# Turning the first chunks of x on TensorE at the head of a fused attention and FFN kernel

## The chip, the cores and the metric

The kernel runs on one core of a Trainium2 chip. The metric is the device time of one execution in microseconds (us). Before the change it is 286.64 us, the median of 3 runs (286.60 to 286.99). The profile below is of one more execution.

## The reference

The input x has 2048 tokens of 640 features. Two branches are computed from it and mixed by a gate for each token. Branch A is a linear attention with 32 heads of width 20; branch B is a gated FFN of width 1728.

```python
x = A_x
g = _sigmoid((x * gate_w).sum(-1, keepdims=True))
# a: q, k, v = x @ wqkv; features of q and k are softmax(p) and softmax(-p), p = q @ w_phi;
#    kv = sum over tokens of features x v; a = (phi_q @ kv) / (phi_q @ z) @ wo
# b: (silu(x @ w_gate) * (x @ w_up)) @ w_down
return g * a + (1 - g) * b
```

All tensors are bfloat16 in HBM. TensorE contracts over the partitions, so both branches need x with its features on the partitions: xT, five chunks of 128 features by 2048 tokens.

## The kernel before

**Tiling.** The tokens are worked in four blocks of 512 (`bt`) for the FFN and in sixteen tiles of 128 (`t`) for the attention. The FFN's 1728 columns are cut into 13 pieces of 128 and one of 64 (`k`). For one block and one piece the gate is five matmuls of 512 columns, one for each chunk of x, into a PSUM bank, and the up part is five more into another. A tail follows: ScalarE computes a tanh of the gate (hT) and a scaled copy of up (us), VectorE combines gate and tanh (L665), POOL multiplies (L671, called hmul). Groups `down` and `rest` then multiply hT with w_down. In the attention a k tile and later a q tile goes through `p1` or `p0` (projection), VectorE's max, min and two subtractions, ScalarE's exp, VectorE's sum and reciprocal, POOL's normalization (L983). For a q tile the features are transposed by a DMA (eT), multiplied with kv (`num`), divided on VectorE (L1066 to L1076), transposed by a DMA (oT) and multiplied with w_o (`wo`). The `rest` group's result is transposed by a DMA too (rX).

**What sets the order.** `_Plan` is a list scheduler that runs while the program is built. Each task has an engine, a cost, a priority, tasks it depends on and pools it takes from (8 PSUM banks among them); a load has a time at which it is said to land. The planner walks through its own time and puts each task on its engine's instruction list when it could start. On the chip each engine then runs its list in order; `_Tracker` adds a semaphore wait where data or a buffer needs one. A task whose cost or landing time is changed can so change the order of others much later. All loads and transposing DMAs stand on one queue, SP's; `load` (with `after`) keeps the loads in the order of their priorities.

**The beginning.** TensorE starts with filler matmuls on a constant (`warm`, L618 to L630): four on banks 0 to 3, then six on banks 4 to 7, 4 and 5. They compute nothing that is used. Then comes the head (`ffn_head`, L694): the gate and up parts of the first four pieces for the first 512 tokens, ordered by what has been loaded rather than piece by piece. Its first group multiplies chunks 0 and 1 of x with four pieces of w_gate, eight matmuls in one task, into four banks; the second does the same with w_up; then come chunks 2 to 4. The loads stand in this order on SP (L547 to L553): w_gate's rows of chunks 0 and 1 for 512 columns; x's chunks 0 and 1 for the first 512 tokens, transposed by the DMA; w_up's rows of chunks 0 and 1; w_gate's rows of chunks 2 to 4 for the first two pieces; x's chunks 2 and 3, and 4, transposed by the DMA; w_gate's other rows; w_up's other rows. POOL meanwhile sets pads and builds masks (L604, L607), and ScalarE loads its table.

Of the kernel before, what the change touches and what calls it, by code (L numbers as in the profile page):

```python
# [6 lines left out]
P = 128  # L7
S_TOK = 2048
D = 640
H = 32  # L10
DH = 20
F_FFN = 1728
NT = S_TOK // P
# [16 lines left out]
NPC_W = 6  # L30
PHI_NH = (6, 6, 6, 6, 6, 2)
ACTF = mybir.ActivationFunctionType
ALU = mybir.AluOpType
AX = mybir.AxisListType
DT = mybir.dt
BF16 = DT.bfloat16
# [204 lines left out]
class _Plan:  # L241
# [11 lines left out]
    def add(self, eng, cost, fn, deps=(), prio=5.0, lat=None, acq=(), rel=(), name=""):  # L253
        t = _Task(eng, cost, fn, deps, prio, self.LAT[eng] if lat is None else lat,
                  tuple(acq), tuple(rel), len(self.tasks), name)
        self.tasks.append(t)
        return t
# [82 lines left out]
def _mm(*cols):  # L340
    return sum(c / 2400.0 + 0.003 for c in cols)


def _build(
# [13 lines left out]
    pe, act, dve, pool, sp = nc.tensor, nc.scalar, nc.vector, nc.gpsimd, nc.sync  # L358
    run = tr.run

    def rowelems(shape):
        r = 1
        for s_ in shape[1:]:
            r *= s_
        return r

    def sb(name, shape, dtype):
        t = nc.alloc_sbuf_tensor(name, list(shape), dtype)
        tr.reg_tensor(t, "sbuf", nc.lookup_mloc(t).addr, rowelems(shape), mybir.dt.size(dtype))
        return t  # L370

    def sbat(name, shape, dtype, at):
        t = nc.alloc_sbuf_tensor_at(name, list(shape), dtype, offset=at)
        tr.reg_tensor(t, "sbuf", at, rowelems(shape), mybir.dt.size(dtype))
        return t

    xT = sb("xT", [P, 5, S_TOK], BF16)
# [33 lines left out]
    base = nc.lookup_mloc(slab).addr  # L411
# [2 lines left out]
    wqT = sbat("wqT", [P, 2 * NPC_W, D], BF16, base)  # L414
    wbd = sbat("wbd", [P, NPC_W, 6, DH], BF16, base + 2 * NPC_W * D * 2)
    wph = sbat("wph", [PC, NPC_W, DH], BF16, base + 2 * NPC_W * D * 2 + NPC_W * 6 * DH * 2)

    ps = nc.alloc_psum_tensor("ps", [P, 8 * 512], F32)
    tr.addr[ps.name] = ("psum", 0, 8 * 512, 4)

    x2 = A_x[0]
# [3 lines left out]
    add = plan.add  # L425
# [4 lines left out]
    def one(b, c0, c1, r0=0, r1=P):  # L430
        return ps[r0:r1, b * 512 + c0:b * 512 + c1]
# [4 lines left out]
    def mms(groups):  # L436

        reads = [g[1] for g in groups] + [g[2] for g in groups]
        writes = []
        seen = set()  # L440
        for g in groups:
            k = (g[0].offset, str(g[0].ap))
            if k not in seen:
                seen.add(k)
                writes.append(g[0])

        def fn():
            last = None
            for o, l, r, st, sp_ in groups:
                last = pe.matmul(o, lhsT=l, rhs=r, start=st, stop=sp_, skip_group_check=True)  # L450
            return last
        run("pe", fn, reads=reads, writes=writes)
# [5 lines left out]
    def actop(o, i, func, scale=1.0):  # L458
        reads = [i] + ([scale] if isinstance(scale, bass.AP) else [])
        run("act", lambda: act.activation(o, i, func, scale=scale), reads=reads, writes=[o])  # L460

    def dveop(fn, reads, writes):
        run("dve", fn, reads=reads, writes=writes)

    def poolop(fn, reads, writes):
        run("pool", fn, reads=reads, writes=writes)

    def memset(t_ap, val, eng):
        eobj = {"pool": pool, "dve": dve}[eng]
        run(eng, lambda: eobj.memset(t_ap, val), reads=[], writes=[t_ap])  # L470
# [3 lines left out]
    def dma(eng, dst, src, transpose=False, keep=False):  # L474
        eobj = tr.engobj[eng]
        reads = [src] if src.tensor.name in tr.addr else []
        writes = [dst] if dst.tensor.name in tr.addr else []
        fn = (lambda: eobj.dma_start(dst, src, transpose=True)) if transpose else (lambda: eobj.dma_start(dst, src))
        ev = run(eng, fn, reads=reads, writes=writes, semname="dma")
        if keep:  # L480
            out_evs.append(ev)
# [12 lines left out]
    def load(eng, dst, src, land, prio, transpose=False, name="load", cost=0.06):  # L494

        t = add(eng, cost, lambda: dma(eng, dst, src, transpose=transpose), prio=prio, lat=2.0, name=name)
        t.land = land
        t.slack = L_SLACK if land > 13 else 0.0
        t.after = chain.get(eng)
        chain[eng] = t  # L500
        return t
# [7 lines left out]
    wgl = [None] * (NPC + 1)  # L509
    wul = [None] * (NPC + 1)  # L510

    def load_gu(j, eng, land, prio):
        c0, c1 = PIECES[j]
        wgl[j] = load(eng, wg[:, :, c0:c1], gsrc[:, :, c0:c1], land[0], prio)
        wul[j] = load(eng, wu[:, :, c0:c1], usrc[:, :, c0:c1], land[1], prio + 0.1)

    def load_x(bt, prio, *cuts):

        tok = slice(512 * bt, 512 * bt + 512)
        out_ = []  # L520
        for i, (c0, c1, land) in enumerate(cuts):
            out_ += [load("sp", xT[:, c0:c1, tok], x2[tok, c0 * P:c1 * P], land, prio + 0.1 * i, True, "x%d" % bt)] * (c1 - c0)
        return out_
# [13 lines left out]
    xs = [None] * NBT  # L537
    HD = 4
    hw = {}

    def load_head(key, c0, c1, k0, k1, land, prio):
        w, src = (wg, gsrc) if key == "g" else (wu, usrc)
        t = load("sp", w[:, c0:c1, k0 * P:k1 * P], src[:, c0:c1, k0 * P:k1 * P], land, prio)
        for k in range(k0, k1):
            hw[key, c0, k] = t
        return t
    load_head("g", 0, 2, 0, HD, 3.9, -43)  # L547
    xa = load_x(0, -42, (0, 2, 5.25))
    load_head("u", 0, 2, 0, HD, 6.9, -41)
    load_head("g", 2, 5, 0, 2, 7.4, -40.5)  # L550
    xs[0] = xa + load_x(0, -40, (2, 4, 8.8), (4, 5, 9.3))
    wgl[0] = load_head("g", 2, 5, 2, HD, 10.0, -39.5)
    wul[0] = load_head("u", 2, 5, 0, HD, 11.3, -39)  # L553
    load_gu(1, "sp", (12.5, 13.7), -37)
    xs[1] = load_x(1, -36.5, (0, 5, 16.4))
    phi_rows = A_w_phi.rearrange("h e f -> (h e) f")
# [16 lines left out]
    xl = [x_[4] for x_ in xs]  # L573

    zero = add("dve", 0.3, lambda: memset(us[:, 0, 0:2], 0.0, "dve"), prio=-20, name="zero")
    table = add("act", 1.3, lambda: actop(us[:, 1, 0:1], us[:, 0, 0:1], ACTF.Tanh), deps=[zero], prio=-20, name="table")
# [39 lines left out]
    def warm(banks, before):  # L618
        ctx = {}

        def fn():
            for b in banks:
                last = pe.matmul(one(b, 0, 512), lhsT=ones_row[:, 0:P], rhs=ones_row[:, 0:512], start=True, stop=True, skip_group_check=True)  # L623
            return last
        b0, b1 = min(banks), max(banks) + 1
        t = add("pe", 0.427 * len(banks), lambda: run("pe", fn, reads=[], writes=[ps[:, b0 * 512:b1 * 512]]), prio=-10,
                acq=[("bank", ctx, i) for i in range(b0, b1)], rel=[("bank", ctx, i) for i in range(b0, b1)], name="warm")
        t.after = before
        return t
    warm_t = warm((4, 5, 6, 7, 4, 5), warm((0, 1, 2, 3), None))  # L630


    gate_t = {}
# [60 lines left out]
    def ffn_head():  # L694
        tsl = slice(0, 512)
        cs = [{} for _ in range(HD)]
        before = warm_t
        last = {}

        def group(key, c0, c1, parts):  # L700
            nonlocal before
            w = wg if key == "g" else wu

            def fn(ks, cc):
                mms([(one(cs[k][key], 0, 512), w[:, c, P * k:P * k + P], xT[:, c, tsl], c == 0, c == 4) for c in cc for k in ks])
            for ks in parts:
                t = add("pe", _mm(*[512] * (len(ks) * (c1 - c0))), lambda ks=ks: fn(ks, range(c0, c1)),
                        deps=[xs[0][c1 - 1], hw[key, min(c0, 2), ks[-1]]], prio=-5,
                        acq=[("bank", cs[k], key) for k in ks] if c0 == 0 else (), name="head")
                t.after = before  # L710
                before = t
                for k in ks:
                    last[key, k] = t
        group("g", 0, 2, [(0, 1, 2, 3)])
        group("u", 0, 2, [(0, 1, 2, 3)])
        group("g", 2, 4, [(0, 1)])
        group("g", 4, 5, [(0, 1)])
        group("g", 2, 5, [(2, 3)])
        group("u", 2, 5, [(0,), (1,), (2,), (3,)])
        for k in range(HD):  # L720
            ffn_tail(0, k, cs[k], (last["g", k], last["u", k]), 0)
# [372 lines left out]
    pre_q = premult(0, wqT_l, PRE_Q, 0.02)  # L1094
    wq_done[0] = pre_q[-1]
    ffn_head()
    for bt in range(NBT):
        for t in range(4 * bt, 4 * bt + 4):
# [5 lines left out]
    for bt in range(1, NBT):  # L1104
        ks = list(range(K_PAIRS if bt == 1 else 0, NK))
# [74 lines left out]
```

## Time and profile before

| | us |
|---|---|
| median of the runs | 286.64 (286.60 to 286.99) |
| the profiled execution's own time | 286.7 |
| its span, from the first to the last instruction | 285.0 |
| TensorE busy in the span | 281.9 (99%) |
| VectorE busy | 225.8 (79%) |
| POOL busy | 172.4 (61%) |
| ScalarE busy | 150.2 (53%) |

The profile is one execution, with times from the span's start. PE is TensorE's matmuls, PEld its weight loads, DVE VectorE, ACT ScalarE, POOL GpSimd, and SPq the issuing of DMAs on SP's queue. A line such as L450 is a line of the kernel; since one helper issues all matmuls, it is the tiles behind it (`ps<-xT,wg`) that tell the groups apart. A matmul is pipelined: its shown duration reaches beyond the start of the next, so that paces are read from start to start. In the first 6.2 us the sixteen DMA engines move 158 GB/s on average.

### The profile page before, as it was taken

The numbers are of one execution on the slowest core, as the hardware profiler recorded it, in microseconds if no ns is written. First come the engines' busy times: TensorE is split into PE (matmuls) and PEld (weight loads), VectorE is DVE, ScalarE is ACT, GpSimd is POOL, SyncE is SP. The second block draws the span as 40 slices with busy tenths as digits, with TensorE's granted clock in tenths as the row PEclk, the third lists the DMA queues.
The fourth block names the chain that finished last, engine by engine and source line by source line (L and its number), as shares of the span: only waits on it lengthen the run. The fifth ranks groups of instructions, "written<-read, shape, count | busy, mean of one in ns | idle before, by whom it ended". The sixth has DMA issues, their size and how long they took to land.

```text
span 285.0 us, 4720 instructions
## 1 busy us (share of the span) xinstructions
PE 281.9 (99%) x1816; PEld 143.4 (50%) x1816; DVE 225.8 (79%) x326; ACT 150.2 (53%) x242; POOL 172.4 (61%) x170
## 2 busy tenths in 40 slices
PE   8999999999999999999999999999999999999996
PEld 3445554555554544555455455455555554554544
DVE  1323449998999797997999999999998989982132
ACT  2455655886676564345761655366655454563210
POOL 5099633749478637366498286588888643867100
PEclk9999999999999999999999999999999999999999
DMA  7979998940000000000002344444344544535211
GB/s 169 264 124 232 231 234 121 307 140 0 0 2 0 2 18 0 2 0 18 2 1 54 74 97 92 100 102 97 74 99 98 116 100 96 69 63 115 48 46 64
DMA packets 70431, 24.73 MB, mean 87 GB/s; under 512 B 58569, under 2 KB 70409, under 8 KB 70409
## 3 DMA queue, kind: packets, MB, share of 16 engines
q1 hardware_dynamic: 69753, 24.43, 40.2%
q8 instruction: 14, 0.23, 0.3%
q10 hardware_dynamic: 656, 0.00, 0.1%
q14 instruction: 8, 0.07, 0.1%
HBM read 8.30 MB, written 2.62 MB: 38 GB/s over the span
## 4 chain that ended last, share of the span: by engine, by line
PE 99%; DVE 0%; issue 0%
PE ps L450 97%; PE ps L623 2%; DVE xsb L760 0%
## 5 line engine op out<-in xcount | busy, mean ns | idle before, releaser
L671 POOL TENSOR_TENSOR hT<-hT,us 128x512 bf16<-128x512 bf16 (+1 forms) x56 | 64.0, 1154 | 52.3 <-DVE hT L665 31.9
L983 POOL TENSOR_TENSOR phi<-phi,rc 128x1320 bf16<-128x1320 bf16 x32 | 77.6, 2426 | 23.6 <-DVE rc L977 23.6
L450 PE MATMUL ps<-xT,wg 128*128 128x512 bf16 x280 | 69.6, 381 | 0.0
L450 PE MATMUL ps<-xT,wu 128*128 128x512 bf16 x260 | 64.3, 379 | 0.0
L665 DVE SCALAR_TENSOR_TENSOR hT<-hT,ps 128x512 bf16<-128x512 bf16 (+1 forms) x56 | 37.6, 677 | 23.4 <-ACT hT L460 23.3
L460 ACT ACTIVATE phi<-phi 128x1320 bf16<-128x1320 bf16 x32 | 41.7, 1303 | 22.6 <-DVE phi L962 22.6
L973 DVE TENSOR_REDUCE sm<-phi 128x66 f32<-128x1320 bf16 x32 | 48.2, 1510 | 5.5 <-ACT phi L460 5.5
L460 ACT ACTIVATE hT<-ps 128x512 bf16<-128x512 f32 (+1 forms) x56 | 33.0, 595 | 37.1 <-PE ps L450 36.9
L450 PE MATMUL ps<-wd,hT 128*128 128x512 bf16 (+2 forms) x238 | 50.7, 366 | 0.0
L450 PE MATMUL ps<-wkv,xT 128*128 128x289 bf16 (+2 forms) x240 | 45.6, 343 | 0.0
L460 ACT ACTIVATE us<-ps 128x512 bf16<-128x512 f32 (+1 forms) x56 | 33.2, 597 | 15.5 <-PE ps L450 13.5
L450 PEld LDWEIGHTS ps<-xT,wu 128*128 128x128 bf16 x260 | 25.4, 98 | 30.7
L450 PEld LDWEIGHTS ps<-xT,wg 128*128 128x128 bf16 x280 | 25.9, 98 | 27.3 <-issue 1.5
L450 PEld LDWEIGHTS ps<-wd,hT 128*128 128x128 bf16 x238 | 22.4, 98 | 24.0
L450 PEld LDWEIGHTS ps<-wkv,xT 128*128 128x128 bf16 x240 | 23.1, 97 | 19.4
L950 DVE TENSOR_REDUCE mx<-ps 128x33 f32<-128x660 f32 x32 | 26.5, 830 | 2.9 <-PE ps L450 2.9
L962 DVE TENSOR_TENSOR phi<-mn,ps 128x660 bf16<-128x660 f32 x32 | 26.6, 831 | 0.5
L954 DVE TENSOR_REDUCE mn<-ps 128x33 f32<-128x660 f32 x32 | 26.5, 829 | 0.0
L958 DVE TENSOR_TENSOR phi<-ps,mx 128x660 bf16<-128x660 f32 x32 | 26.4, 825 | 0.0
L460 ACT ACTIVATE xsb<-ps,gs 128x512 bf16<-128x512 f32 (+1 forms) x16 | 11.9, 741 | 27.3 <-PE ps L450 27.2
L450 PE MATMUL ps<-wq,xT 128*128 128x512 bf16 (+1 forms) x160 | 24.3, 299 | 0.0
L450 PE MATMUL ps<-wo,oT 128*128 128x512 bf16 (+1 forms) x160 | 24.2, 299 | 0.0
(52 smaller groups left out, 208.9 us busy)
## 6 DMA issues: line engine op xcount, KB each, us to landing
out_dram<-xsb SPq DMA_DIRECT2D x15, 160.0 KB, 1.8
wd<-in_B_w_down_dram SPq DMA_DIRECT2D x1, 2080.0 KB, 10.1
wg<-in_B_w_gate_dram SPq DMA_DIRECT2D x2, 400.0 KB, 6.1
wu<-in_B_w_up_dram SPq DMA_DIRECT2D x2, 400.0 KB, 6.4
wo<-in_A_wo_dram SPq DMA_DIRECT2D x1, 800.0 KB, 10.6
wg<-in_B_w_gate_dram SPq DMA_DIRECT2D x2, 320.0 KB, 5.2
wu<-in_B_w_up_dram SPq DMA_DIRECT2D x2, 320.0 KB, 5.8
wkv<-in_A_wqkv_dram SPq DMA_DIRECT2D x1, 600.0 KB, 5.0
```

Of the source, the lines that this page charges most:

```text
L450: last = pe.matmul(o, lhsT=l, rhs=r, start=st, stop=sp_, skip_group_check=True)
L460: run("act", lambda: act.activation(o, i, func, scale=scale), reads=reads, writes=[o])
L623: last = pe.matmul(one(b, 0, 512), lhsT=ones_row[:, 0:P], rhs=ones_row[:, 0:512], start=True, stop=True, skip_group_check=True)
L665: dveop(lambda: dve.scalar_tensor_tensor(out=hap, in0=hap, scalar=1.0, in1=g_, op0=ALU.add, op1=ALU.mult), [hap, g_], [hap])
L671: poolop(lambda: pool.tensor_tensor(hap, hap, u_, ALU.mult), [hap, u_], [hap])
L950: dveop(lambda: dve.tensor_reduce(a, b, AX.X, ALU.max), [b], [a])
L954: dveop(lambda: dve.tensor_reduce(a, b, AX.X, ALU.min), [b], [a])
L958: dveop(lambda: dve.tensor_tensor(o_, a, b, ALU.subtract), [a, mx[:, ctx["st"], :]], [o_])
L962: dveop(lambda: dve.tensor_tensor(o_, a, b, ALU.subtract), [b, mn[:, ctx["st"], :]], [o_])
L973: dveop(lambda: dve.tensor_reduce(a, b, AX.X, ALU.add), [b], [a])
L983: poolop(lambda: pool.tensor_tensor(a, a, b, ALU.mult), [a, r], [a])
```

## The change

The first load on SP is now x's chunks 0 and 1 for the first 512 tokens as they lie in HBM (xp: 128 partitions, four tiles of tokens, 256 features, 256 KB, in runs of 512 bytes), by a plain DMA. The transposing DMA of these two chunks is gone. The other loads follow in the old order; w_gate's rows of chunks 0 and 1 are still one transfer, now the second.

POOL builds a 128x128 identity first of all. After the fillers TensorE turns xp: for each of the two chunks four matmuls with a tile of xp as the weights and the identity as the 128 columns that move, two of them into one bank and two into another. VectorE copies the first bank (256 columns) to xT, ScalarE the second. The fillers go from ten to seven. In the head the first w_gate group becomes two of four matmuls, one for each chunk, and each waits for its chunk's two copies instead of the transposing DMA. The times at which the planner takes the head's loads to land are changed too.

```diff
+    xp = sbat("xp", [P, 4, 2 * P], BF16, tbase)
+    ident = sbat("ident", [P, P], BF16, tbase + 8 * P * 2)
...
-    load_head("g", 0, 2, 0, HD, 3.9, -43)
-    xa = load_x(0, -42, (0, 2, 5.25))
-    load_head("u", 0, 2, 0, HD, 6.9, -41)
-    load_head("g", 2, 5, 0, 2, 7.4, -40.5)
-    xs[0] = xa + load_x(0, -40, (2, 4, 8.8), (4, 5, 9.3))
-    wgl[0] = load_head("g", 2, 5, 2, HD, 10.0, -39.5)
-    wul[0] = load_head("u", 2, 5, 0, HD, 11.3, -39)
+
+    xp_l = load("sp", xp[:, :, :], x2[0:512, 0:2 * P].rearrange("(t p) j -> p t j", p=P), 3.7, -43)
+    load_head("g", 0, 2, 0, HD, 4.6, -42)
+    load_head("u", 0, 2, 0, HD, 5.5, -41)
+    load_head("g", 2, 5, 0, 2, 6.2, -40.5)
+    xs[0] = [None, None] + load_x(0, -40, (2, 4, 7.6), (4, 5, 8.2))
+    wgl[0] = load_head("g", 2, 5, 2, HD, 9.3, -39.5)
+    wul[0] = load_head("u", 2, 5, 0, HD, 10.6, -39)
...
+    def build_ident():
+        memset(ident[:, :], 1.0, "pool")
+        for m, b in ((1, 0), (-1, 0)):
+            poolop(lambda m=m: pool.affine_select(
+                out=ident[:, :], in_=ident[:, :], pattern=[[-m, P]], compare_op=ALU.is_ge, fill=0.0,
+                base=0, channel_multiplier=m), [ident[:, :]], [ident[:, :]])
+    ident_t = add("pool", 0.8, build_ident, prio=-30, name="ident")
...
-    warm_t = warm((4, 5, 6, 7, 4, 5), warm((0, 1, 2, 3), None))
+    warm_t = warm((4, 5, 6, 7), warm((0, 1, 2), None))
+
+    def turn(c, before):
+        ctx = {}
+
+        def fn():
+            mms([(one(ctx[i // 2], P * (i % 2), P * (i % 2) + P), xp[:, i, c * P:(c + 1) * P], ident[:, :], True, True) for i in range(4)])
+        t = add("pe", 0.43, fn, deps=[xp_l, ident_t], prio=-10, acq=[("bank", ctx, 0), ("bank", ctx, 1)], name="turn")
+        t.after = before
...
+        ev.append(add("dve", 0.36, copy_d, deps=[t], prio=-30, rel=[("bank", ctx, 0)], name="turned"))
+        ev.append(add("act", 0.36, copy_a, deps=[t], prio=-30, rel=[("bank", ctx, 1)], name="turned"))
+        return t, ev
+    turn_t, xe0 = turn(0, warm_t)
+    turn_t, xe1 = turn(1, turn_t)
+    xe = [xe0, xe1]
...
-        before = warm_t
+        before = turn_t
...
-                        deps=[xs[0][c1 - 1], hw[key, min(c0, 2), ks[-1]]], prio=-5,
+                        deps=(xe[c1 - 1] if c1 < 3 else [xs[0][c1 - 1]]) + [hw[key, c0, ks[-1]]], prio=-5,
...
-        group("g", 0, 2, [(0, 1, 2, 3)])
+        group("g", 0, 1, [(0, 1, 2, 3)])
+        group("g", 1, 2, [(0, 1, 2, 3)])
         group("u", 0, 2, [(0, 1, 2, 3)])
```

More of the change, by code (lines that the diff above doesn't have):

```diff
@@ L416, in _build @@
     wph = sbat("wph", [PC, NPC_W, DH], BF16, base + 2 * NPC_W * D * 2 + NPC_W * 6 * DH * 2)
+    tbase = base + -(-(2 * NPC_W * D * 2 + NPC_W * 7 * DH * 2) // 32) * 32
+    assert tbase % 32 == 0 and tbase + 10 * P * 2 <= base + NT * D * 2, tbase
+    xp = sbat("xp", [P, 4, 2 * P], BF16, tbase)
+    ident = sbat("ident", [P, P], BF16, tbase + 8 * P * 2)
     ps = nc.alloc_psum_tensor("ps", [P, 8 * 512], F32)
@@ L539, in _build, with load_head @@
     hw = {}
-    def load_head(key, c0, c1, k0, k1, land, prio):
+    def load_head(key, c0, c1, k0, k1, land, prio, eng="sp"):
         w, src = (wg, gsrc) if key == "g" else (wu, usrc)
-        t = load("sp", w[:, c0:c1, k0 * P:k1 * P], src[:, c0:c1, k0 * P:k1 * P], land, prio)
-        for k in range(k0, k1):
-            hw[key, c0, k] = t
-        return t
-    load_head("g", 0, 2, 0, HD, 3.9, -43)
-    xa = load_x(0, -42, (0, 2, 5.25))
-    load_head("u", 0, 2, 0, HD, 6.9, -41)
-    load_head("g", 2, 5, 0, 2, 7.4, -40.5)
-    xs[0] = xa + load_x(0, -40, (2, 4, 8.8), (4, 5, 9.3))
-    wgl[0] = load_head("g", 2, 5, 2, HD, 10.0, -39.5)
-    wul[0] = load_head("u", 2, 5, 0, HD, 11.3, -39)
+        t = load(eng, w[:, c0:c1, k0 * P:k1 * P], src[:, c0:c1, k0 * P:k1 * P], land, prio, cost=0.06 if eng == "sp" else 0.45)
+        for c in range(c0, c1):
+            for k in range(k0, k1):
+                hw[key, c, k] = t
+        return t
+    xp_l = load("sp", xp[:, :, :], x2[0:512, 0:2 * P].rearrange("(t p) j -> p t j", p=P), 3.7, -43)
[5 more added lines that the diff above has]
+    wul[0] = load_head("u", 2, 5, 0, HD, 10.6, -39)
     load_gu(1, "sp", (12.5, 13.7), -37)
@@ L629, in warm, with half, copy_d, copy_a @@
         return t
-    warm_t = warm((4, 5, 6, 7, 4, 5), warm((0, 1, 2, 3), None))
+    warm_t = warm((4, 5, 6, 7), warm((0, 1, 2), None))
[5 more added lines that the diff above has]
+        t.after = before
+        ev = []
+        def half(h):
+            return xT[:, c, 256 * h:256 * h + 256], one(ctx[h], 0, 256)
+        def copy_d():
+            o_, i_ = half(0)
+            dveop(lambda: dve.tensor_copy(o_, i_), [i_], [o_])
+        def copy_a():
+            o_, i_ = half(1)
+            actop(o_, i_, ACTF.Copy)
+        ev.append(add("dve", 0.36, copy_d, deps=[t], prio=-30, rel=[("bank", ctx, 0)], name="turned"))
[4 more added lines that the diff above has]
+    xe = [xe0, xe1]
     gate_t = {}
```

## The prediction

> **What bounds the kernel.** I read the chain of work that ended last first, then TensorE's waits, then the first microseconds in order of time.
>
> ```profile
> PE 99%; DVE 0%; issue 0%
> PE ps L450 97%; PE ps L623 2%; DVE xsb L760 0%
> ```
> ```profile
> PE ps L623 <- PEq L1164: 0.8, 1, 0.8
> ```
>
> The first two lines are the shares of the span on the chain: it is TensorE (PE) nearly alone. The third is the whole answer of the view of waits for that engine: it waits 0.8 us for the start and never again. I checked this by the starts of its groups: after the first 7 us every group of one shape takes the same time as any other group of that shape, up to the end of the last matmul at 282.8. So the end moves by what TensorE's own stream gains or loses, and by any wait that is new in it. What other engines or queues save is worth nothing.
>
> The stream's beginning (start us, us, engine, line, operation, count):
>
> ```profile
> 0.84 4.43 PE L623 MATMUL ps<-const-bfloat16-1.0 128*128 128x512 bf16 x10 [0.84 <-PEq L1164]
> 5.10 2.41 PE L450 MATMUL ps<-xT,wg 128*128 128x512 bf16 x8
> 7.35 1.89 PE L450 MATMUL ps<-xT,wu 128*128 128x512 bf16 x8
> 9.07 2.75 PE L450 MATMUL ps<-xT,wg 128*128 128x512 bf16 x12
> ```
> ```profile
> 5.07 0.15 PEld L450 LDWEIGHTS ps<-xT,wg 128*128 128x128 bf16 x2 [0.70 <-issue]
> 5.49 0.15 PEld L450 LDWEIGHTS ps<-xT,wg 128*128 128x128 bf16 x1 [0.28 <-issue]
> 5.92 0.15 PEld L450 LDWEIGHTS ps<-xT,wg 128*128 128x128 bf16 x1 [0.28 <-issue]
> 6.27 0.75 PEld L450 LDWEIGHTS ps<-xT,wg 128*128 128x128 bf16 x4 [0.20 <-issue]
> ```
>
> From start to start, ten filler matmuls take 4.26 us, 0.426 each; the eight of the second w_up group 1.72, 0.215 each. So the engine begins at half pace (the row of granted clock says 9 tenths all the same) and changes inside the first real group: of its eight, n are slow, 0.426 n + 0.215 (8 - n) = 2.25, n = 2.5, and the change is at 5.10 + 2.5 x 0.426 = 6.17. The weight loads, 0.43 apart until 5.92 and then closer, say the same.
>
> The queue that feeds it:
>
> ```profile
> 0.80 0.45 SPq L478 DMA_DIRECT2D wg<-in_B_w_gate_dram  x1
> 1.31 1.31 SPq L478 DMA_TRANSPOSE xT<-in_A_x_dram  x1
> 2.69 0.56 SPq L478 DMA_DIRECT2D wu<-in_B_w_up_dram  x1
> ```
> ```profile
> wg<-in_B_w_gate_dram SPq DMA_DIRECT2D x1, 256.0 KB, 3.0
> xT<-in_A_x_dram SPq DMA_TRANSPOSE x1, 3.6
> ```
>
> The last number is us from issue to landing: w_gate's piece is there at 3.80, the transposed x at 4.91. The fillers end at 0.84 + 4.26 = 5.10: x comes inside them, and the ten fillers are what sets the head's start.
>
> **The change, part by part.**
>
> *Fillers, 10 to 7.* They end at 0.84 + 7 x 0.426 = 3.82.
>
> *x's transfer at the front.* It has the size of w_gate's piece, which landed in 3.0 us from the same place, in runs of 512 bytes where that has 1,024. A later piece with 512-byte runs (192 KB, issued at 3.29 behind others) took 3.7. Bounds 3.80 to 4.50; I take 3.80, the row from the same place, because the piece with short runs landed only 0.6 us after the 256 KB ahead of it (6.99 and 6.39), which is no slower a pace. The turns also wait for the identity: one memset (0.21) and two selects (0.35 each, by the mask's rows at L604 and L607) after 0.80, done near 2. That moves POOL's masks by 0.9 us, in front of 8.9 us of idle time; without that cover it would delay hmul.
>
> *Eight turns, 128 columns.* At a quarter of 512 columns and half pace 0.107 each, 0.43 for each chunk. Upper bound 0.147 each, the slow weight load; the lower row is the twelve 120-column matmuls of the premultiply, 0.59 us in all although a weight load takes 0.098, so loads are covered. I take 0.107. The turns run from 3.82 to 4.68.
>
> *Copies, a new wait.* The last matmul of chunk 0 starts at 4.14. In the head a reader started 0.42 after the start of its last matmul (9.07 + 5 x 0.215 = 10.15, and 10.57), 0.20 beyond the streaming; here 0.107 + 0.20, so copies start at 4.45. For 256 columns ScalarE's rows of 512 (0.60) and 640 (0.70) give 0.40, and VectorE's copies of 320 (0.48), 384 (0.49) and 640 (0.83) bound it by 0.3 and 0.48; I take 0.42. A hand-over of 0.03 (hT at L460 to L665) to 0.2; I take 0.08. The first head matmul can start at 4.95, between 4.75 and 5.15 if x is on time. Behind this wait stands all of TensorE; from 4.68 it idles 0.27. Both copying engines are free: their next work was at 10.57 and 11.20. Chunk 1's copies end near 5.4, under chunk 0's four matmuls (1.7 at half pace).
>
> *w_gate's piece second.* Issued at 1.31, it needs 256 KB more at the pace of 192 KB in 0.60: 3.80 + 0.80 = 4.6, under 4.95. If the copies were faster it would be next. Later pieces: a plain issue (0.51) replaces one that held SP for 1.38, so everything from w_up on is issued some 0.85 us earlier, and the bytes are the same. The tightest in before, w_up's later chunks (issued 7.02 + 4.2 = 11.2, used at 11.66), has 0.4 to spare and loses only the 0.1 by which it is used earlier.
>
> *Order.* The plan comes out otherwise: gates 4 and 5 run before ups 4 and 5, and from the second FFN half on (about 170 us) groups change places. These are the same matmuls, so the stream's sum stays.
>
> *Sum.* If the pace changes at 6.17 again, the head runs slow from 4.95 to 6.17: 1.22 / 0.426 = 2.9 matmuls; the other 5.1 take 1.10. The second group starts at 7.27 instead of 7.35: **-0.08 us**. Three fillers (1.28) are saved, turns (0.86) and the wait (0.27) eat 1.13, and half of the rest is lost since it is slow time. Ends: head at 4.75, -0.16; x at 4.50 so head at 5.65, +0.28; breaks that put off the pace change by as much as they last, another +0.2. The profiled execution took 286.7 (span 285.0 and 1.7 around it), 0.06 over the median of 286.64. So 286.6, and 286.4 to 287.2 within this case.
>
> **Rivals.**
>
> *The pace changes much later (slower).* Before, TensorE ran without a break for 5.33 us until the change. After, it has a break of about 0.27 at 4.7, perhaps one at 3.8. If a break starts the count again, the change comes at 4.95 + 5.33 = 10.28: 12.5 head matmuls are slow instead of 2.5, 10 x 0.211 = 2.11, less 0.15 for the earlier start: +1.96, 288.7. It decides from the shortest break that counts, which no row shows. Against it: turns and fillers fill about nine tenths of the time up to 6.17. [...] Chance 0.16.
>
> *The pace changes early (faster).* The trace also fits a count of matmuls: 12.5 before the change. The turns bring that count at 3.82 + 5.5 x 0.107 = 4.41. All eight of the head then take 1.72 from 4.95: next group at 6.67, -0.68, 286.0. [...] Chance 0.15.
>
> *A new wait in the reordered part.* In before the shortest way from a num group to its wo group is
>
> ```profile
> 156.97 0.48 PE L450 MATMUL ps<-kvsb,eT 128*128 128x63 bf16 x11
> 164.15 1.52 PE L450 MATMUL ps<-wo,oT 128*128 128x512 bf16 x10
> ```
>
> 6.85 us of other matmuls, without a wait. After, tile 9 has 6.2 (wo, p0, wo and one FFN pair), and on SP the transposition of the rest (rX) now stands ahead of its oT. From the end of num: rX is issued at about 0.5 and holds SP for 1.48, 2.0; the quotient is ready at 2.3 to 2.7; oT lands in 2.6 to 3.8: 4.9 to 6.5, and with ScalarE late by one exp (1.30) up to 7.4. TensorE would wait 0 to 1.1; middle 0.6, 287.2. All other such ways are 6.85 or more, and from p0 to num none is under 19.6 (before: 18.6). Chance 0.15, half of it beyond the bound below.
>
> *It doesn't bring x earlier*: the long end of x's landing, +0.28, inside the forecast.
>
> **How the numbers follow.** Forecast 0.54, late change 0.16, early change 0.15, new wait 0.15. The range takes in the forecast, the early change and nearly all of the wait: 285.9 to 287.7; outside is the late change. A measurement tells about 0.2% (0.57 us) from no change. Within it: 0.54 + 0.07 = 0.61; slower 0.16 + 0.08 = 0.24; faster 0.15.
>
> **What would show it.** Seven fillers, turns from about 3.8, first w_gate group near 4.95, w_up group near 7.3; weight loads 0.43 apart until about 6.2. Slow matmuls beyond 7 us show the late change, none in the head the early one; any TensorE wait after 10 us shows the reordering. A first turn after 4.3 means that I mis-sized x's landing.

## The result, and the profile after

The changed kernel takes **286.90 us** (median of 22 runs, 286.55 to 287.49) against 286.44 for the kernel before in the same sessions (22 runs, 286.08 to 286.99): a ratio of 1.0016, 95% interval 1.0010 to 1.0022. It is 0.46 us slower, clear of the noise, though within the 0.2% that I had called no change; I had forecast 0.08 us less. The profiled execution (287.20 us) has a span of 285.4 us, 0.5 longer than before's (285.44 against 284.95).

The chain of the changed kernel (shares of the span by engine and by line), and the view of TensorE's waits:

```profile
PE 98%; issue 1%; DVE 0%
PE ps L454 97%; PE ps L637 1%; DVE xT L660 0%; DVE xsb L801 0%
```
```profile
PE ps L637 <- PEq L1205: 0.8, 1, 0.8
PE ps L454 <- DVE xT L660: 0.2, 1, 0.2
```

Still TensorE alone, and only one wait more than before, that for the copies. The beginning, first TensorE's groups, then its weight loads, then the two leading transfers with the us to landing:

```profile
0.84 3.15 PE L637 MATMUL ps<-const-bfloat16-1.0 128*128 128x512 bf16 x7 [0.84 <-PEq L1205]
3.95 1.04 PE L454 MATMUL ps<-ident,xp 128*128 128x128 bf16 x8
5.17 2.21 PE L454 MATMUL ps<-xT,wg 128*128 128x512 bf16 x8 [0.18 <-DVE xT L660]
7.22 1.89 PE L454 MATMUL ps<-xT,wu 128*128 128x512 bf16 x8
8.95 2.75 PE L454 MATMUL ps<-xT,wg 128*128 128x512 bf16 x12
```
```profile
5.14 0.13 PEld L454 LDWEIGHTS ps<-xT,wg 128*128 128x128 bf16 x2 [0.42 <-issue]
5.55 0.15 PEld L454 LDWEIGHTS ps<-xT,wg 128*128 128x128 bf16 x1 [0.28 <-issue]
5.92 0.96 PEld L454 LDWEIGHTS ps<-xT,wg 128*128 128x128 bf16 x5 [0.23 <-issue]
```
```profile
xp<-in_A_x_dram SPq DMA_DIRECT2D x1, 256.0 KB, 3.1
wg<-in_B_w_gate_dram SPq DMA_DIRECT2D x1, 256.0 KB, 3.3
```

The second group starts at 7.22, 0.13 ahead of before's 7.35, and the third at 8.95 against 9.07. So at 9 us the changed kernel leads by 0.12. Its last matmul, however, starts at 283.05 against 282.57. Some 0.60 us are lost on the way.

The view of waits doesn't show where, because a matmul's shown duration (0.379 us for 512 columns) reaches past the start of the next one (0.216 later) and covers short gaps. I compared starts instead: each step from one matmul to the next with the usual step for its columns. (33 matmul records are missing, 1,788 against 1,821 weight loads, which makes a step longer by just one matmul of 0.215; those are set aside.) Three steps are too long by something else: 0.21 at 200.4, 0.25 at 227.4 and 0.15 at 237.7, 0.61 in all, and none in before. Here are the three places in the changed kernel's order of time. The first:

```profile
196.81 0.48 PE L454 MATMUL ps<-kvsb,eT 128*128 128x63 bf16 x11
198.12 1.29 ACT L464 ACTIVATE phi<-phi 128x1320 bf16<-128x1320 bf16 x1
199.43 0.60 ACT L464 ACTIVATE hT<-ps 128x512 bf16<-128x512 f32 x1
199.93 0.59 ACT L464 ACTIVATE us<-ps 128x512 bf16<-128x512 f32 x1
200.57 0.76 PEld L454 LDWEIGHTS ps<-xT,wu 128*128 128x128 bf16 x5 [0.54 <-ACT us L464]
```

The last line's bracket says it: the up part waits for ScalarE's us copy, which reads the PSUM bank that the up part is to write. That copy ends at 200.52; an exp of 1.29 us stands ahead of it and of its tanh. The first line, a num group, will matter further on. The second and third:

```profile
224.25 2.42 POOL L1024 TENSOR_TENSOR phi<-phi,rc 128x1320 bf16<-128x1320 bf16 x1 [0.71 <-DVE rc L1018]
225.53 1.29 DVE L821 SCALAR_TENSOR_TENSOR xsb<-rX,gs,xsb 128x128 bf16<-128x128 bf16 x1
226.74 0.67 DVE L705 SCALAR_TENSOR_TENSOR hT<-hT,ps 128x512 bf16<-128x512 bf16 x1
227.53 1.37 PEld L454 LDWEIGHTS ps<-wq,xT 128*128 128x128 bf16 x10 [0.23 <-issue]
...
236.23 0.78 DVE L1003 TENSOR_TENSOR phi<-mn,ps 128x660 bf16<-128x660 f32 x1
236.93 0.83 DVE L1117 TENSOR_TENSOR ob<-ps,rd 128x660 bf16<-128x660 f32 x1
237.87 1.37 PEld L454 LDWEIGHTS ps<-wo,oT 128*128 128x128 bf16 x10 [0.45 <-issue]
```

At 227.5 TensorE's next projection starts 0.1 after the end of VectorE's stt (L705, which combines gate and tanh; its end, 227.41, frees a bank); stt is late because a small addition ahead of it took 1.29 us, and that addition ends 0.15 after a long POOL instruction. At 237.9 `wo` starts 0.1 after the end of the division (ob, 237.76), which frees a pair of banks.

### The profile page after: what moved, and what is told of

Read it like the earlier page. It is cut to its first block, busy times and chain, and to the rows that moved or that the text cites. A ratio compares the mean times of both kernels' runs of the same rounds, so it can differ in the third digit from the quotient of the medians.

```text
span 285.4 us, 4693 instructions
## 1 busy us (share of the span) xinstructions
PE 280.4 (98%) x1788; PEld 143.5 (50%) x1821; DVE 227.9 (80%) x328; ACT 150.6 (53%) x244; POOL 173.0 (61%) x173
## 4 chain that ended last, share of the span: by engine, by line
PE 98%; issue 1%; DVE 0%
PE ps L454 97%; PE ps L637 1%; DVE xT L660 0%; DVE xsb L801 0%
## 5 line engine op out<-in xcount | busy, mean ns | idle before, releaser
L454 PE MATMUL ps<-xT,wg 128*128 128x512 bf16 x269 | 67.2, 380 | 0.7 <-DVE xT L660 0.2
L454 PE MATMUL ps<-xT,wu 128*128 128x512 bf16 x256 | 63.6, 379 | 0.3
L705 DVE SCALAR_TENSOR_TENSOR hT<-hT,ps 128x512 bf16<-128x512 bf16 (+1 forms) x56 | 37.5, 676 | 21.5 <-ACT hT L464 21.4
L454 PE MATMUL ps<-wd,hT 128*128 128x512 bf16 (+2 forms) x233 | 49.9, 367 | 0.2
L454 PE MATMUL ps<-wq,xT 128*128 128x512 bf16 (+1 forms) x157 | 23.7, 298 | 0.2
L454 PE MATMUL ps<-wo,oT 128*128 128x512 bf16 (+1 forms) x154 | 23.4, 296 | 0.3
```

Source lines behind the costliest of these rows:

```text
L705: dveop(lambda: dve.scalar_tensor_tensor(out=hap, in0=hap, scalar=1.0, in1=g_, op0=ALU.add, op1=ALU.mult), [hap, g_], [hap])
```

## The experiments

Theory A: the new head gains a little, and what is lost are three waits of TensorE for PSUM banks in the part whose order the planner changed. Theory B: the head itself costs the time. Ratios are to the kernel before, on the same chip, with 95% intervals.

**The head and the order, each by itself.** The planner's landing times alone were set, so that all engines' lists behind the head are exactly before's (first edit, on the changed kernel) or exactly the changed kernel's (second, on the kernel before).

```diff
-    load_head("u", 0, 2, 0, HD, 5.5, -41)
+    load_head("u", 0, 2, 0, HD, 6.9, -41)
...
+    for e in xe0 + xe1:
+        e.land = 5.25
```
```diff
-    xa = load_x(0, -42, (0, 2, 5.25))
+    xa = load_x(0, -42, (0, 2, 4.96))
...
-        t = add("pe", 0.427 * len(banks),
+        t = add("pe", 0.41 * len(banks),
```

New head, old order:

> The changed head (x untransposed first, seven fillers, eight turns), but the planner is told the old landing times, so that every engine's list behind the head is that of the kernel before. Theory A (the 0.46 us come from three new waits of TensorE in the reordered part, 0.21 + 0.25 + 0.15 us by the trace of the changed kernel, while its head ends 0.12 us earlier): no wait of TensorE after 10 us, 0.1 us faster than before, ratio 0.9996 (0.9990 to 1.0002). Theory B (the new head itself costs the time, for example by a later change of pace in most runs, and the profiled execution was a lucky one): as slow as the changed kernel, ratio near 1.0016.

286.43 against 286.61, ratio 0.9993 (0.9985 to 1.0002); no lengthened step after 10.1 us.

Old head, new order:

> The kernel before with its old head (ten fillers, x transposed by the DMA), but the planner is told the new landing times, so that every engine's list behind the head is that of the changed kernel. Theory A: the same three waits of TensorE near 200, 227 and 238 us, 0.6 us slower than before, ratio 1.0021 (1.0012 to 1.0028). Theory B: as before, ratio 1.0000 (0.9994 to 1.0006).

287.09 against 286.61, ratio **1.0018** (1.0009 to 1.0027). The same three steps are longer, by 0.21, 0.26 and 0.15, in TensorE's weight loads of this kernel:

```profile
200.51 0.33 PEld L450 LDWEIGHTS ps<-xT,wu 128*128 128x128 bf16 x3 [0.54 <-ACT us L460]
```
```profile
227.47 0.34 PEld L450 LDWEIGHTS ps<-wq,xT 128*128 128x128 bf16 x3 [0.24 <-issue]
```
```profile
237.81 0.13 PEld L450 LDWEIGHTS ps<-wo,oT 128*128 128x128 bf16 x2 [0.45 <-issue]
```

Theory B falls: the loss goes with the order, without any of the new instructions. The first kernel was run once more on another chip:

> The changed head with the old order once more, on this chip: ratio to before 0.9993 again (0.9988 to 0.9998), no wait of TensorE after 12 us. It is to tell whether the head by itself gains a tenth of a us. If the head were worth nothing, 1.0000 (0.9995 to 1.0005).

286.25 against 286.42, ratio 0.9995 (0.9986 to 1.0004). Both times 0.17 to 0.18 us are gained, and both intervals include 1: the head's gain is likely, and not shown.

**Taking the three waits away.** Tasks are put on the lists in planned order as before, but after the planning one task moves behind another on its engine.

```diff
+        for e, i, j in MOVES:
+            own = [t for t in emit if t.eng == e]
+            a, b = own[i], own[j]
+            emit.remove(a)
+            emit.insert(emit.index(b) + 1, a)
+        for t in emit:
+            t.fn()
...
+MOVES = (('act', 171, 173), ('dve', 256, 257), ('dve', 269, 270))
```

> The changed kernel with three instructions moved in their engine's list: an exp of ScalarE behind the tanh and us that follow it (near 198 us), one 128-column addition of the rest on VectorE behind the stt that follows it (near 225.5 us), one subtraction on VectorE behind the division (o) that follows it (near 236 us). Theory A: each frees a PSUM bank before TensorE asks for it, the three waits go, and nothing else becomes late: 0.6 us less than the changed kernel, ratio to before 0.9996 (0.9990 to 1.0004). Theory B: the waits go or not, the time stays near ratio 1.0016. A third way: the moved instructions make something else late, and new waits of some tenths take their place.

287.25 us, ratio 1.0022 (1.0013 to 1.0031): the third way. The three waits are gone, and 0.85 us of others are there: 0.03, 0.11 and 0.16 between 213 and 216.4, and 0.55 at 239, where a moved subtraction made an exp late, which stands ahead of the evacuation (ScalarE's copy out of PSUM, xb) that frees the next pair:

```profile
237.51 1.30 ACT L475 ACTIVATE phi<-phi 128x1320 bf16<-128x1320 bf16 x1 [2.51 <-DVE phi L1014]
238.72 0.67 ACT L475 ACTIVATE xb<-ps,gs 128x512 bf16<-128x512 f32 x1
...
239.44 0.55 PEld L465 LDWEIGHTS ps<-wq,xT 128*128 128x128 bf16 x4 [0.55 <-ACT xb L475]
```

So each move was made alone. The exp:

> The changed kernel with the first of the three moves alone: the exp of ScalarE behind the tanh and us that follow it near 198 us. Theory A (each wait has one late release of a PSUM bank behind it): the wait of 0.21 us at 200 goes, those of 0.25 and 0.15 at 227 and 238 stay. The three moves together brought waits of 0.03, 0.11 and 0.16 between 213 and 217 us; these lie ahead of the other two moves, so they should be here too: 0.09 us worse than the changed kernel, 0.70 us of waits. Theory C (there is no slack of some tenths in this part at all, and any move only passes the wait on): the same sum of waits, 0.6, at other places.

287.22, ratio 1.0030 (1.0018 to 1.0041). The wait at 200 is gone; 0.15 at 215, 0.17 at 216, 0.35 at 227.6 and 0.14 at 238 make 0.80: theory A in kind, though the waits are larger than it said. The up part at 215.2 waits for a us again, and an exp ahead of that us starts at 212.88 instead of the changed kernel's 212.48. How the moved exp makes this one late I did not follow through.

The addition:

> The changed kernel with the second move alone: the 128-column addition of the rest on VectorE, which took 1.29 us beside a running POOL instruction, behind the stt that follows it near 225.5 us. Theory A: stt ends before 226.5, the wait of 0.25 us at 227.3 goes and nothing takes its place: 0.36 us of waits are left, 0.25 us faster than the changed kernel. The addition, begun later beside the same POOL instruction, ends with it again and takes some 0.3 to 0.6. Theory C: a wait of about 0.25 us comes up behind it.

286.45 against 286.42, ratio **1.0003** (0.9994 to 1.0012): one instruction moved by one place takes back nearly all of the loss. Not only the wait at 227 is gone but that at 238 too, which I had not expected; 0.21 at 200 is left. In this kernel's order of time the addition, started later, is held for a shorter while, and stt is ahead of it:

```profile
223.81 2.42 POOL L1035 TENSOR_TENSOR phi<-phi,rc 128x1320 bf16<-128x1320 bf16 x1 [0.71 <-DVE rc L1029]
...
225.26 0.69 DVE L716 SCALAR_TENSOR_TENSOR hT<-hT,ps 128x512 bf16<-128x512 bf16 x1
...
225.87 0.51 DVE L832 SCALAR_TENSOR_TENSOR xsb<-rX,gs,xsb 128x128 bf16<-128x128 bf16 x1
```

The subtraction:

> The changed kernel with the third move alone: a subtraction on VectorE behind the division (o) near 236 us. Theory A: the wait of 0.15 us at 237.6 goes, but the subtraction's exp is 0.8 us later and stands ahead of the evacuation on ScalarE that frees the next pair of banks: the wait of 0.55 us at 239 that the three moves brought is here too, 0.4 us slower than the changed kernel, 1.0 us of waits. If that wait came from the second move, it is not here, and the kernel is 0.15 us faster than the changed one.

287.85, ratio 1.0051 (1.0035 to 1.0066): the wait at 237.7 is gone, and 0.79 at 239.4 has come, behind the same evacuation; 1.25 of waits in all, theory A with a larger wait than the 0.55 it named.

**What held the addition.**

```diff
-            poolop(lambda: pool.tensor_tensor(a, a, b, ALU.mult), [a, r], [a])
+            if t == 11 and not which:
+                d = dst()
+                for _ in range(2):
+                    poolop(lambda: pool.memset(d, 0.0), [d, r], [d])
+            else:
+                poolop(lambda: pool.tensor_tensor(a, a, b, ALU.mult), [a, r], [a])
```

> The changed kernel, but for q tile 11 POOL's normalization of the features (2.42 us, reads and writes SBUF; it ran when VectorE's addition of the rest took 1.29 us instead of 0.34) is replaced by two memsets of the same tile, some 1.25 us each, which only write; so this tile's output is not computed. Theory D (the addition, which reads two tensors of SBUF, waits for a POOL instruction that reads SBUF): the addition takes 0.34 us beside the memset, the waits of TensorE at 227 and 238 us go as they do when the addition is moved behind stt, 0.2 us of waits are left, ratio to before 1.0003. Rival E (any POOL instruction on SBUF holds it): the addition starts near 225.5 in the second memset and ends with it, 1.2 us later; the waits of 0.25 and 0.15 us stay, ratio 1.0016.

In order of time, with one place later in the same kernel:

```profile
224.62 2.45 POOL L1027 MEMSET phi<- 128x1320 bf16 x2 [0.69 <-DVE rc L1018]
...
225.92 0.34 DVE L821 SCALAR_TENSOR_TENSOR xsb<-rX,gs,xsb 128x128 bf16<-128x128 bf16 x1
```
```profile
240.10 2.43 POOL L1029 TENSOR_TENSOR phi<-phi,rc 128x1320 bf16<-128x1320 bf16 x1
240.29 2.38 DVE L821 SCALAR_TENSOR_TENSOR xsb<-rX,gs,xsb 128x128 bf16<-128x128 bf16 x1 [0.27 <-ACT xsb L464]
```

Beside a memset the addition takes 0.34, and the waits at 227 and 238 are gone (the 0.21 at 200 stays): theory E falls, and D fits. The time is nevertheless 288.11, ratio 1.0050 (1.0037 to 1.0064): another of the eight additions now started 0.19 after a normalization and was held for nearly all of it, 2.38 us; VectorE's next instructions came late by it, and TensorE waited 1.43 at 245. I had not foreseen that; it is the same hold once more, 2.04 us longer than the 0.34 beside the memset.

**The change of pace.** Three fillers, with the new head and the old order:

```diff
-    warm_t = warm((4, 5, 6, 7), warm((0, 1, 2), None))
+    warm_t = warm((0, 1, 2), None)
```

> The changed head with the old order and only three fillers, so that TensorE stands still from 2.1 us until x lands at 3.9. If a break starts the count for the change of pace again (the rival of the prediction), the pace changes some 5.3 us after 5.2, near 10.5 us, and the time is 2.0 us over that of seven fillers, ratio 1.007. [...] If breaks of this length don't count, the pace changes near 6 us as with seven fillers: ratio 0.9996.

288.04, ratio 1.0046 (1.0031 to 1.0061), 1.6 us over the same kernel with seven. In the profiled execution:

```profile
3.83 1.03 PE L454 MATMUL ps<-ident,xp 128*128 128x128 bf16 x8 [1.54 <-POOL kvm L474]
5.04 3.04 PE L454 MATMUL ps<-xT,wg 128*128 128x512 bf16 x8 [0.18 <-DVE xT L660]
7.91 1.89 PE L454 MATMUL ps<-xT,wu 128*128 128x512 bf16 x8
```

Six of the eight head matmuls are slow (0.43 us from start to start, 0.215 afterwards) and the pace changes at 7.4, 3.6 us after the turns begin: later than in any profile with seven fillers, and not by a restart at the head, which gives 10.5. But this execution was the fastest of the four (287.25 to 288.49), so that the median stands, if nothing else differs, for a later change. All four lie above all eleven runs with seven fillers (286.18 to 286.88): a standstill of 1.75 us does put the change off. The interval leaves out both a count that starts again at the head (1.007) and a break that doesn't count (0.9996); a count that starts again at the turns is not excluded.

**A transfer on another queue.** In the two profiles of the new head with the old order (the second on the other chip) the pace changed early, before 5.1 us, and TensorE then waited 0.25 and 0.13 us near 9.7 for w_gate's later rows. So these were issued by ScalarE:

```diff
-    wgl[0] = load_head("g", 2, 5, 2, HD, 10.0, -39.5)
+    wgl[0] = load_head("g", 2, 5, 2, HD, 10.0, -15, "act")
...
+    wgl[0].hold = 1.4
```

> The changed head with the old order, and w_gate's rows of chunks 2 to 4 for pieces 2 and 3 (192 KB) are issued by ScalarE near 2.3 us instead of by SP behind two transposing DMAs near 6.4 us. Where the pace changes early, TensorE waits 0.13 to 0.25 us for this transfer at 9.6 us. If its place in SP's queue is what makes it late: it lands before 8, the wait goes, 0.1 to 0.2 us less than the changed head with the old order, ratio to before 0.9988 (0.9980 to 0.9996). Rival: the transfers of the first 10 us share the DMA engines, and what it gains w_up's rows or x's chunks lose: a wait for one of these between 6 and 9.5 us in its place, ratio 0.9994 or more.

286.59 against 286.51, ratio 1.0010 (0.9995 to 1.0024): the rival, with other losers than I had named. The transfer was not issued near 2.3 but at once, 0.17 us after x's piece:

```profile
0.97 0.42 ACTq L482 DMA_DIRECT2D wg<-in_B_w_gate_dram  x1
```

It landed at 4.65, where it had landed at 9.85 and 10.05 from SP's queue. x's piece landed after 3.5 us instead of 2.9 to 3.1, and w_gate's first piece at 5.41 instead of 4.4 to 4.6, so that the turns began at 4.31 and the head at 5.53. There was no wait near 9.7 in its profiled execution, but there the pace changed only at 6.3, when none is to be expected; so what the other place would save where the pace changes early stays open, and so does an issue near 2.3.

No version here is shown to be faster than the kernel before.

## Why the prediction was wrong

*What bounds the kernel*: right. Every difference found is one of TensorE's own stream.

*Fillers, x's transfer, turns, copies*: near. x landed 3.1 us after its issue (3.0 taken), so that the turns began at 3.95; they went at 0.107 each. The copies started 0.35 after the start of their last turn (0.31 taken) and took 0.42 at most, as forecast; the hand-over took 0.15 instead of 0.08. The head started at 5.17 in the profiled execution, at 4.96 to 5.11 in the seven other seven-filler profiles of the table below whose loads were unchanged; I had said 4.95. The wait for w_gate's piece wasn't next, as predicted.

*"Everything from w_up on is issued some 0.85 us earlier"*: true of the first ones (w_up at 1.86 instead of 2.69), but not of those behind the transposing DMAs. w_gate's later rows, issued at 6.40 before, were issued at 5.85 in the changed kernel and at 6.46 to 6.54 in three of the four profiles with seven fillers that changed pace at 5.1 or earlier. There they, and not w_up's later chunks, were what TensorE waited for. In the fourth (the addition) they were issued at 6.00 and landed at 9.45, and no wait came.

*"If the pace changes at 6.17 again"*: wrong as an assumption, small in effect. In twelve profiled executions, counting from the same start at 0.84, the pace changed at

| kernel | us |
|---|---|
| ten fillers: before; old head, new order | 6.2; 4.0 |
| seven: changed; new head, old order, twice | 5.9; 4.6 to 5.1; 4.5 to 5.0 |
| seven: three moves; exp; addition; subtraction | 4.15; 5.9; 5.1; 5.8 |
| seven: memsets; load on ScalarE | 6.7; 6.3 |
| three | 7.4 |

The two ten-filler kernels have the same head, and so do the seven-filler ones but for the load on ScalarE; yet they changed at different times. So it is a matter of the execution more than of the kernel, although the one kernel that was profiled twice changed at about the same time both times. Apart from the three fillers the rows spread over 2.7 us, and no run shows what sets the moment. What an early change gives is partly taken back by waits for data: the old head waited 0.7 for x when the pace changed at 4.0, the new one 0.13 to 0.25 for w_gate near 9.7 (0.42 with the three moves). So the late change and the early change that I set up as rivals of the change, with 0.16 and 0.15, are neither: breaks of 0.3 to 0.6 us did not restart anything (no profile with seven fillers changed after 6.7, where a new count from the head, by the 3.1 us that the shortest one took, gives 8.1 or more), and a count of matmuls does not fit 4.0 and 6.2 with the same ten fillers. They may be what makes runs of one kernel differ; with a profile or two of each that isn't shown.

*"These are the same matmuls, so the stream's sum stays"*: this is the step that failed. The sum of the matmuls stayed, and the waits between them didn't: 0.61 us. I had a rival for it, "a new wait in the reordered part", with a middle of 0.6 us, which is the size that came; but I gave it 0.15, and it came at other places and by another path, so that the size is luck. I had followed only the ways through the transposing DMAs (tile 9's num to wo). That one held: oT was issued at 221.5 and `wo` ran at 225.95 without a wait. What I didn't follow is how PSUM banks come free: by ScalarE's us, VectorE's stt and its division. For each of these the question was what stands ahead of it on its engine's list. The two orders side by side would have told of two. Before's order at the same two places:

```profile
196.74 1.31 ACT L460 ACTIVATE phi<-phi 128x1320 bf16<-128x1320 bf16 x1 [1.44 <-DVE phi L962]
198.01 1.24 PE L450 MATMUL ps<-xT,wu 128*128 128x512 bf16 x5
199.03 1.22 ACT L460 ACTIVATE us<-ps 64x512 bf16<-64x512 f32 x2
199.09 0.48 PE L450 MATMUL ps<-kvsb,eT 128*128 128x63 bf16 x11
200.49 1.24 PE L450 MATMUL ps<-xT,wu 128*128 128x512 bf16 x5
```
```profile
225.74 0.68 DVE L665 SCALAR_TENSOR_TENSOR hT<-hT,ps 128x512 bf16<-128x512 bf16 x1
227.97 0.37 DVE L780 SCALAR_TENSOR_TENSOR xsb<-rX,gs,xsb 128x128 bf16<-128x128 bf16 x1
```

The exp stood ahead of that us in before too. But there a num group ran between the two up parts, which gave the us 0.32 us more before TensorE asked for its bank: it ended at 200.25, and the up part began at 200.49. In the changed kernel num stands ahead of both (196.81), and the up part would have begun at 200.37, before the us ended. (This is read from the two orders; num was not moved by itself.) The second place is plainer: the addition had stood behind stt and moved in front of it. A subtraction stood ahead of the division in both orders; that third wait follows from VectorE being late, since it goes with the one at 227 when only the addition is moved or freed of its hold.

The second thing that no planner's cost in this kernel contains is the hold between VectorE and POOL. The addition costs the planner 0.25; it took 1.29. It began 1.28 us into POOL's normalization and ended 0.15 after it. By the experiments this one hold of 0.95 us is behind two of the three waits, 0.40 of 0.61, although the second comes ten us later. The first, at 200, comes from the planned order without any hold; the one move that was tried against it, the exp's, took it away and delayed other things by more.

The sum then closes: 0.61 of waits less the 0.17 of the two head runs (which is likely and not shown) is 0.44, and 0.46 was measured. The new order by itself cost 0.48 with the old head, 0.26 to 0.77 by its interval, which holds the 0.61. The range held the time, the sign was wrong.

## What to carry to other kernels

A kernel whose bound engine never waits is balanced on its order: a change worth a tenth of a microsecond at the head can be outweighed by the new order that a planner makes of it, so keep the order fixed when you judge such a change. For each group that moves, look not only at its inputs but at which instruction frees its buffer, and at what now stands ahead of that instruction. Where the view of waits is empty, compare start-to-start steps and the idle time in the weight loads' rows.

## What the runs showed of the hardware that I had not expected

VectorE's 128x128 addition, with two tensors of SBUF as inputs (rX and xsb), takes 0.24 to 0.35 us when nothing holds it. Started while POOL's tensor-tensor ran, it did not end until POOL's had: it took 1.29 us in the changed kernel, 0.51 where it was moved behind stt, 2.38 in the kernel with the memsets, and 0.37 in before, and each time it ended 0.14 to 0.15 after POOL's. Beside POOL's memset it took 0.34. The stt, which has one of its two inputs in PSUM, took 0.69 beside the same normalization and 0.68 beside the memset. Which feature of the two instructions makes the hold, no run shows. In before's trace the 0.37 beside a POOL multiplication is the only sign of a hold.
